# The first MoE's weight chunks in twos: one tile, one join and one check of 768 columns

## The chip, the core and the metric

The kernel runs on one core of one Trainium2 chip. The metric is the device time of one execution in microseconds (us), as the median over several runs. The engines are named as in the profile: PE is TensorE's matmuls, PEld its weight loads, DVE is VectorE, ACT ScalarE, POOL GpSimd and SP SyncE, which issues the transfers.

## The reference

Three stages follow each other: a gated linear attention, a first MoE with an RMS norm and a gated hidden layer, and a second MoE with a maximum of three products. The weights and `alpha` come as float64.

```python
for t in range(S):                       # S = 768, 4 x 8 heads of 48
    state = alpha[:, :, t, :, None] * state + np.einsum('bhd,bhe->bhde', k[:, :, t], v[:, :, t])
    y[:, :, t] = np.einsum('bhd,bhde->bhe', q[:, :, t], state)
...
xn = x / rms * rms_g                     # x: 3072 tokens of 384
g = xn @ w_gate                          # w_gate, w_val: 384 x 1536
silu = g * (1.0 / (1.0 + np.exp(-g)))
x = silu * (xn @ w_val) @ w_out          # w_out: 1536 x 384
...
h = np.maximum(np.maximum(x @ w1, x @ w2), x @ w3)   # 384 x 768 each
out = h @ w_out                          # 768 x 384
```

## The kernel before

**Attention.** The tokens are cut into 24 tiles of 128, worked on as a chunked recurrence. The first six tiles have `k`, `q` and `alpha` turned by PE (L579), the later ones by DVE (L585). A tile's *decay block* on DVE is the COPY `all`, a MEMSET, the scan `R`, `least` and `kT` (L604 to L613); later come `starts`, `aT`, `qT` (L617 to L630), the masked scores `at` (L666), the normed rows `xn` (L719) and the low half `xl` of the turned rows (L736), which with `xh` is what the first MoE reads.

**The first MoE** has 96 slots, each one block of 384 tokens by one hidden block of 128 columns. A slot is a gate product `g` (9 matmuls, L769), a value product `v` (L769), the silu on ACT into `sg` (L799), the multiply on DVE (L802), the high half `hh` on ACT (L806), the low half `hl` on DVE (L810) and the second product `s` on PE (L816). The first slots take hidden blocks 0 to 5 for token blocks 0 and 1, so the weights of a hidden block are wanted soon after the first gate. Every product is made of three matmuls of halves: high x high, high x low, low x high.

**The weights.** The class `Weights` cuts them into chunks of 128 partitions x 384 columns, three chunks (gate, value, out) for each hidden block, 36 for the first MoE (tag `w1`) and 24 for the second (`w2`). A chunk is loaded as int64 into a tile `raw` (L360, queue of SP), *joined* into a float32 tile `cv_t` by three integer operations on DVE (L58, L59, L60), split into a high half by a copy on ACT (L374) and a low half, the *rest*, by a subtraction on DVE (L380: `wgl`, `wvl`, `wol`), and *checked* on ACT by two activations with sums over the row (L389, L392, each with the read of its accumulator). Joins go two chunks at a time: `zip` over the two generators interleaves their operations.

```python
def join(nc, raw, t, n):
    yield nc.vector.tensor_scalar(bits, up, 3, TOP2 + 1, ALU.logical_shift_left, ALU.bitwise_or)
    yield nc.vector.scalar_tensor_tensor(bits, up, BELOW, bits, ALU.bitwise_or, ALU.bitwise_and)
    yield nc.vector.scalar_tensor_tensor(bits, low, 29, bits, ALU.logical_shift_right, ALU.bitwise_or)
```

**The order** of the instructions on each engine comes from the class `Order`. Every part is added with an engine, a cost, a due time (in slots), the parts that it needs, and the instructions that it issues. `run` plays the parts through: each engine that is free takes the ready part with the earliest due time, and is busy for the part's cost. The order in which the parts start is the order in the program. On PE, filler matmuls (L776) are put in where nothing is ready, until the first value product. So a cost that is changed can move any part of any engine against the others. For `w1` the raw tiles have four buffers: a load waits for the check and the join of the chunk four back.

Of the kernel before, what the change touches and what calls it, by code (L numbers as in the profile page):

```python
# [11 lines left out]
F32 = mybir.dt.float32  # L12
F32R = mybir.dt.float32r
BF16 = mybir.dt.bfloat16
I32 = mybir.dt.int32
U32 = mybir.dt.uint32
I64 = mybir.dt.int64
AF = mybir.ActivationFunctionType
# [7 lines left out]
P = 128  # L26
# [3 lines left out]
NF1 = F1 // P  # L30
# [16 lines left out]
def words(raw, n):  # L47

    bits, floats = (raw.bitcast(t).rearrange("p (n w) -> p n w", w=2) for t in (I32, F32))
    return bits[:, :n, 1], floats[:, :n, 1], bits[:, :n, 0]  # L50
# [231 lines left out]
def gla_moe_moe(ctx: ExitStack, tc: tile.TileContext, q, k, v, alpha, wg, wv, wo, g, w1, w2, w3, wo2, out):  # L282
    nc = tc.nc
# [5 lines left out]
    const = ctx.enter_context(tc.tile_pool(name="const", bufs=1))  # L289
    NSTAT = 4  # L290
    CW = 384
    tiles = [(b, c) for c in range(NC) for b in range(B)]
    nw = sum(w.shape[0] * w.shape[1] for w in (wg, wv, wo, w1, w2, w3, wo2)) // (P * CW)
    stats = const.tile([P, len(tiles) * NSTAT + nw], F32, name="stats")
    nc.gpsimd.memset(stats, 0.0)
    small = const.tile([P, nw], F32, name="small")
    nc.gpsimd.memset(small, 0.0)
    bound = const.tile([P, 1], F32, name="bound")
# [6 lines left out]
    NT = len(tiles)  # L305
# [3 lines left out]
    pp = work.enter_context(tc.tile_pool(name="pp", bufs=1, space=PSUM))  # L309
    banks = [pp.tile([P, 512], F32, name=f"bank{i}") for i in range(8)]  # L310
    mp = work.enter_context(tc.tile_pool(name="mp", bufs=2, side="left"))
    junk = const.tile([P, 512], BF16, name="junk")
    plan = Order()

    def bank(i, rows, a, n):
# [6 lines left out]
    class Weights:  # L322


        def __init__(self, tag, pool, bufs, chunks, where, due, needs):

            self.tag, self.pool, self.raws, self.tmps = tag, pool, {}, {}
            self.chunks, self.where = chunks, where
            n = len(chunks)
            first = tag == "w1"  # L330
            for i in range(n):
                at = due(i) - 10 - (HEAD[i // 2] if first and i < 8 else 1.5)
                before = needs(i) + self.prev("load", i, 1) + self.prev("check", i, bufs)
                if i >= bufs:
                    before.append((tag, "join", (i - bufs) // 2 * 2))
                plan.add((tag, "load", i), "SP", 1.1, at, before, partial(self.load, i, bufs), later=LAT)
            for i in range(0, n, 2):
                both = [j for j in (i, i + 1) if j < n]
                at = due(i) - (HEAD[i // 2] if first and i < 8 else 1 if first else 1.5)
                plan.add((tag, "join", i), "DVE", 1.3 * len(both), at,  # L340
                         [(tag, "load", j) for j in both] + self.prev("rest", i, 2) + self.prev("join", i, 2),
                         partial(self.join, both))
                plan.add((tag, "high", i), "ACT", 0.45 * len(both), at, [(tag, "join", i)] + self.needed(needs, both),
                         partial(self.high, both))
                plan.add((tag, "rest", i), "DVE", 0.47 * len(both), at + 0.2, [(tag, "high", i)],
                         partial(self.low, both))
                for j in both:
                    plan.add((tag, "check", j), "ACT", 1.42, at + 2, [(tag, "load", j)],
                             partial(self.check, j))

        def prev(self, kind, i, n):
            return [(self.tag, kind, i - n)] if i >= n else []
# [2 lines left out]
            return []  # L355

        def load(self, i, bufs):
            raw = self.pool().tile([P, CW], I64, name="raw", bufs=bufs)
            src, shape = self.chunks[i]
            nc.sync.dma_start(out=raw.rearrange("p (a b) -> p a b", a=shape[0]), in_=src)  # L360
            self.raws[i] = raw

        def join(self, both):
            steps = []
            for i in both:
                self.tmps[i] = self.pool().tile([P, CW], F32, name="cv_t", bufs=2)
                steps.append(join(nc, self.raws[i], self.tmps[i], CW))
            for _ in zip(*steps):
                pass
# [11 lines left out]
                    dl, self.tmps.pop(i).rearrange("p (a b) -> p a b", a=a), dh.bitcast(F32), ALU.subtract  # L381
                )

        def check(self, i):

            n = seen[0]
            seen[0] += 1
            col = NT * NSTAT + n
            nc.scalar.activation(  # L389
                junk[:, :CW], words(self.raws[i], CW)[1], AF.Square, scale=2.0**34, accum_out=stats[:, col:col + 1]  # L390
            )
            nc.scalar.activation(  # L392
                junk[:, :CW], junk[:, :CW], AF.Relu, scale=-(2.0**22), bias=bound, accum_out=small[:, n:n + 1]
            )

        def ready(self, i):
# [36 lines left out]
    for nm, fill in (("al", 1.0), ("kk", 0.0), ("qq", 0.0)):  # L433
        t = ap1.tile([P, 2 * H * 64], F32, name=f"in_{nm}")
# [352 lines left out]
    for s, (blk, f, pi) in enumerate(slots):  # L787
# [43 lines left out]
        if f == f1 - 1:  # L831
            for e in range(KT):
# [14 lines left out]
                before = [("yst", pi - 1, e)] if pi else []  # L847
                if f0:
                    plan.add(("yld", pi, e), "SP", 0.55, s - 1, before + [("yst", pi - 2, e), ("g", s - 1)] +
                             ([("yld", pi, e - 1)] if e else []), fetch, later=2.2)  # L850
                    before = [("yld", pi, e)]
# [51 lines left out]
        return tuple(w_[:, :, cols(f)] for w_ in w2s[kind])  # L903

    n = len(chunks1)
    done_att = [("t", "el", NT - 1), ("t", "sqb", NT - 1), ("w1", "check", n - 1), ("w1", "rest", n - 2)]

    class Weights2(Weights):
        def needed(self, needs, both):
# [8 lines left out]
    for blk in range(PLAIN):  # L918
# [5 lines left out]
        at = NS + (blk - 1) * NF2 + 1 if blk else NS - 6  # L924
# [7 lines left out]
        for i in range(KT):  # L932
# [8 lines left out]
            n = blk * KT + i  # L941
# [3 lines left out]
    for z in range(NZ):  # L945
# [31 lines left out]
        before = [("m", z - 1, 1) if z else ("mu", NS - 1), ("m", z - 1, 2) if z else None]  # L977
# [90 lines left out]
    for n in range(NS1):  # L1068
        fp, j = divmod(n, 3)
        at = NS + 3 + 0.5 * n  # L1070
# [6 lines left out]
        at = NS + 10.5 + 0.1 * n  # L1077
# [13 lines left out]
    for sb in range(1, NBLK // 2):  # L1091
# [211 lines left out]
        for late in range(2):  # L1303
            for t in range(2 * TPB):
# [18 lines left out]
                at = at0 + 8.4 + 0.33 * t + (2 * late)  # L1323
# [73 lines left out]
```

## Time and profile before

| | us |
|---|---|
| median of 3 runs | 892.62 (892.55 to 892.76) |
| the profiled execution | 892.83 |
| its span in the trace | 891.0 |
| PE busy | 871.4 (98%) |
| DVE busy | 639.5 (72%) |
| ACT busy | 363.6 (41%) |

The span runs from the first to the last instruction of the trace; what the run takes beyond it lies outside the trace. The granted clock of TensorE is given as a share of full speed. In rows of one engine's time line, the first number is the start in us from the span's start, the second the time from there to the end of the row's last instruction; x2 stands for two instructions in one row. A bracket at the end of a row is the idle time of the engine just before it and what ended it.

### The profile page before, as it was taken

What the parts mean: (1) busy time and instruction counts of PE and PEld (TensorE: products, weight loads), DVE (VectorE), ACT (ScalarE), POOL (GpSimd) and SP (SyncE); (2) the same over time, 40 slices, a digit from 0 to 9 for tenths busy, and PEclk for the clock granted to TensorE, in tenths of its full rate; (3) what the DMA queues carried; (4) which work ended last, traced back from release to release, by engine and by line L of the source; (5) the groups of instructions that cost most, each with busy time, mean ns of one, the idle gap of its engine ahead of it and who ended that gap; (6) DMA issues with size and microseconds to landing.
All of it is one profiled execution on the core that took longest, in us unless ns stands there. A gap on an engine that the chain in (4) does not pass through costs nothing.

```text
span 891.0 us, 16476 instructions
## 1 busy us (share of the span) xinstructions
PE 871.4 (98%) x6446; PEld 848.2 (95%) x6446; DVE 639.5 (72%) x1321; ACT 363.6 (41%) x928; POOL 22.1 (2%) x66
## 2 busy tenths in 40 slices
PE   7999899999999999999999999999999999999996
PEld 6889898999999999999999999999999999999996
DVE  8999999997666666666665367559886874865780
ACT  4578776433223333333233267645333232224121
POOL 1000000000000000000000000000000000000000
PEclk9999999999999999999999999999999999999998
DMA  9835654353222223222221025321200011011001
GB/s 201 190 105 175 194 164 139 86 142 85 56 53 77 53 50 81 52 53 80 58 59 51 5 85 178 107 94 49 81 1 28 1 54 54 1 53 54 1 1 56
DMA packets 106244, 69.17 MB, mean 78 GB/s; under 512 B 49200, under 2 KB 103856, under 8 KB 106160
## 3 DMA queue, kind: packets, MB, share of 16 engines
q1 hardware_dynamic: 106160, 68.05, 28.0%
q8 instruction: 52, 0.85, 0.4%
q14 instruction: 32, 0.26, 0.1%
HBM read 57.41 MB, written 10.62 MB: 76 GB/s over the span
## 4 chain that ended last, share of the span: by engine, by line
PE 86%; DVE 6%; DMA 3%; ACT 2%; SPq 2%; issue 1%; DVEq 0%; ACTq 0%
PE bank L769 35%; PE bank L1085 17%; PE bank L816 15%; PE bank L1313 6%; PE bank L653 2%; PE bank L691 2%; PE bank L776 2%; PE bank L972 2%; DMA raw<-in_moe_w_out_dram 1%; PE bank L685 1%; PE bank L676 1%; PE bank L725 1%; SPq L562 1%; DVE cv_t L59 1%; SPq L551 1%
## 5 line engine op out<-in xcount | busy, mean ns | idle before, releaser
L802 DVE TENSOR_TENSOR sg<-sg,bank 128x384 f32<-128x384 f32 x96 | 53.0, 552 | 95.7 <-PE bank L769 95.1
L806 ACT ACTIVATE hh<-sg 128x384 fp32r<-128x384 f32 x96 | 50.0, 521 | 149.0 <-DVE sg L802 148.9
L769 PE MATMUL bank<-xh,wgh 128*128 128x384 f32 x288 | 100.7, 349 | 1.5 <-ACT sg L799 1.5
L816 PE MATMUL bank<-hh,woh 128*128 128x384 f32 x288 | 98.0, 340 | 0.0
L816 PE MATMUL bank<-hl,woh 128*128 128x384 f32 x288 | 96.6, 335 | 1.3 <-DVE hl L810 1.2
L769 PE MATMUL bank<-xl,wgh 128*128 128x384 f32 x288 | 96.7, 336 | 1.2 <-DVE xl L736 1.2
L769 PE MATMUL bank<-xh,wgl 128*128 128x384 f32 x288 | 96.9, 336 | 0.2 <-DVE wgl L380 0.2
L769 PE MATMUL bank<-xh,wvh 128*128 128x384 f32 x288 | 96.7, 336 | 0.0
L769 PE MATMUL bank<-xh,wvl 128*128 128x384 f32 x288 | 96.4, 335 | 0.0
L816 PE MATMUL bank<-hh,wol 128*128 128x384 f32 x288 | 96.3, 334 | 0.0
L769 PE MATMUL bank<-xl,wvh 128*128 128x384 f32 x288 | 96.2, 334 | 0.0
L810 DVE TENSOR_TENSOR hl<-sg,hh 128x384 fp32r<-128x384 f32 x96 | 53.4, 556 | 31.0 <-ACT hh L806 30.9
L799 ACT ACTIVATE sg<-bank 128x384 f32<-128x384 f32 x96 | 46.7, 486 | 38.0 <-PE bank L769 36.9
L769 PEld LDWEIGHTS bank<-xh,wgh 128*128 128x128 f32 x288 | 54.1, 188 | 3.4 <-ACT sg L799 1.8
L816 PEld LDWEIGHTS bank<-hl,woh 128*128 128x128 f32 x288 | 54.1, 188 | 2.2 <-DVE hl L810 2.2
L816 PEld LDWEIGHTS bank<-hh,woh 128*128 128x128 f32 x288 | 54.0, 188 | 1.9
L769 PEld LDWEIGHTS bank<-xl,wgh 128*128 128x128 f32 x288 | 54.2, 188 | 1.5 <-DVE xl L736 1.5
L769 PEld LDWEIGHTS bank<-xh,wgl 128*128 128x128 f32 x288 | 54.1, 188 | 0.9 <-DVE wgl L380 0.9
L769 PEld LDWEIGHTS bank<-xh,wvh 128*128 128x128 f32 x288 | 54.1, 188 | 0.5 <-DVE sg L802 0.5
L769 PEld LDWEIGHTS bank<-xl,wvh 128*128 128x128 f32 x288 | 54.1, 188 | 0.0
L769 PEld LDWEIGHTS bank<-xh,wvl 128*128 128x128 f32 x288 | 54.1, 188 | 0.0
L816 PEld LDWEIGHTS bank<-hh,wol 128*128 128x128 f32 x288 | 54.0, 188 | 0.0
(252 smaller groups left out, 2058.0 us busy)
## 6 DMA issues: line engine op xcount, KB each, us to landing
raw<-in_moe_w_out_dram SPq DMA_DIRECT2D x18, 384.0 KB, 3.6
raw<-in_moe_w_dram SPq DMA_DIRECT2D x18, 384.0 KB, 3.8
y_scr<-yo SPq DMA_DIRECT2D x30, 192.0 KB, 1.9
raw<-in_moe_w_gate_dram SPq DMA_DIRECT2D x12, 384.0 KB, 4.2
vt<-in_v_dram SPq DMA_DIRECT2D x24, 192.0 KB, 2.6
raw<-in_moe_w_val_dram SPq DMA_DIRECT2D x12, 384.0 KB, 4.6
out_dram<-yo SPq DMA_DIRECT2D x24, 192.0 KB, 1.9
in_al<-in_alpha_dram SPq DMA_DIRECT2D x36, 96.0 KB, 2.2
```

The lines of the kernel that those rows point to most:

```text
L653: nc.tensor.matmul(self.sc[i][:, pr, :], self.kT[lo:hi, pr, :], self.qT[lo:hi, pr, :], start=True, stop=True)
L691: nc.tensor.matmul(self.y[tk, 2 * pr + i, :], at[i][:, pr, tk], vt[:, 2 * pr + i, :], start=not self.c, stop=True, skip_group_check=True,)
L769: nc.tensor.matmul(ps, w_[:, kt, col], m_[:, kt, :], start=i == 0, stop=i == 3 * KT - 1)
L776: nc.tensor.matmul(banks[4][:, 0:2 * P], ident.bitcast(BF16)[:, 0:P], mask.bitcast(BF16), start=True, stop=True)
L799: nc.scalar.activation(hid[s], banks[3][:, :NB], AF.Silu)
L802: nc.vector.tensor_tensor(hid[s], hid[s], banks[4][:, :NB], ALU.mult)
L806: nc.scalar.activation(hi_[s], hid[s], AF.Copy)
L810: nc.vector.tensor_tensor(lo_[s], hid.pop(s), hi_[s].bitcast(F32), ALU.subtract)
L816: nc.tensor.matmul(banks[e][:, :NB], w_[:, f, es], m_, start=f == f0 and i == 0, stop=f == f1 - 1 and i == 2)
L972: nc.tensor.matmul(banks[t][:, :DM], l_[:, tsl], r_[:, f, :], start=f == 0 and i == 0, stop=f == NF2 - 1 and i == 2)
L1085: nc.tensor.matmul(ps, l, r, start=start and i == 0, stop=i == 2, skip_group_check=True)
L1313: nc.tensor.matmul(banks[i][:, :DM], l, r[:, f, :], start=f == 0 and m_ == 0, stop=f == NF2 - 1 and m_ == 2)
```

## The change

For `w1` alone (`self.wide`), two chunks are loaded into the halves of one raw tile of 768 columns, of which there are two instead of four of 384. One join of three operations over 768 columns writes one `cv_t` of 768 columns, and one check runs over 768 columns. The copies to the high halves and the rests stay at 384. The first load of a pair waits for the check and the join of the pair before the last, the second load only for the first. The planner's cost of a pair's join goes from 2.6 to 2.25, that of its checks from 2 x 1.42 to 2.2, and the check waits for both loads. The tables of sums, `stats` and `small`, have 18 columns fewer. Lines behind L313 move down, from L360 on by 13 to 20 (L380 becomes L400, L604 becomes L624, L810 becomes L830).

```diff
+    nw -= NF1 * 3 // 2
...
-    junk = const.tile([P, 512], BF16, name="junk")
+    junk = const.tile([P, 2 * CW], BF16, name="junk")
...
-            first = tag == "w1"
+            first = self.wide = tag == "w1"
...
-                before = needs(i) + self.prev("load", i, 1) + self.prev("check", i, bufs)
+                before = needs(i) + self.prev("load", i, 1)
+                if not self.wide or i % 2 == 0:
+                    before += self.prev("check", i, bufs)
...
-                plan.add((tag, "join", i), "DVE", 1.3 * len(both), at,
+                plan.add((tag, "join", i), "DVE", 2.25 if self.wide else 1.3 * len(both), at,
...
+                if self.wide:
+                    plan.add((tag, "check", i), "ACT", 2.2, at + 2, [(tag, "load", j) for j in both],
+                             partial(self.check, i, 2 * CW))
+                    continue
...
+                if i % 2 == 0:
+                    self.raws[i] = self.pool().tile([P, 2 * CW], I64, name="raw", bufs=bufs // 2)
+                raw = self.raws[i - i % 2][:, i % 2 * CW:(i % 2 + 1) * CW]
...
+            if self.wide:
+
+                t = self.pool().tile([P, 2 * CW], F32, name="cv_t", bufs=1)
+                for _ in join(nc, self.raws[both[0]], t, 2 * CW):
+                    pass
+                for n, i in enumerate(both):
+                    self.tmps[i] = t[:, n * CW:(n + 1) * CW]
+                return
```

Two places in the order of DVE. The first is the start of the program, from the first tile's `qT` on; x2 stands for two equal rows, here one of each chunk. In before:

```order
L630 TENSOR_TENSOR qT<-bank_75,aT 112x512
L58 TENSOR_SCALAR cv_t<-raw 128x384 x2
L59 SCALAR_TENSOR_TENSOR cv_t<-raw,cv_t 128x384 x2
L60 SCALAR_TENSOR_TENSOR cv_t<-raw,cv_t 128x384 x2
L666 TENSOR_TENSOR at<-bank_78,mask 128x512
L666 TENSOR_TENSOR at<-bank_79,mask 128x512
L604 COPY all<-bank_80 112x4
L605 MEMSET bank_80 112x4
```

In the change, at the same place (L400 is the rest):

```order
L650 TENSOR_TENSOR qT<-bank_75,aT 112x512
L58 TENSOR_SCALAR cv_t<-raw 128x768
L59 SCALAR_TENSOR_TENSOR cv_t<-raw,cv_t 128x768
L60 SCALAR_TENSOR_TENSOR cv_t<-raw,cv_t 128x768
L686 TENSOR_TENSOR at<-bank_78,mask 128x512
L686 TENSOR_TENSOR at<-bank_79,mask 128x512
L400 TENSOR_TENSOR wgl<-cv_t,wgh 128x3x128
L400 TENSOR_TENSOR wvl<-cv_t,wvh 128x3x128
L624 COPY all<-bank_80 112x4
L625 MEMSET bank_80 112x4
```

The six operations of the join have become three, each reading the one before it, and the two rests of the first pair, which stood further back, have moved ahead of the second tile's decay block.

The second place is around the eleventh `hl` of the first MoE (slot 10), some 120 us into the span. In before, from that `hl` on:

```order
L810 TENSOR_TENSOR hl<-sg,hh 128x384
L380 TENSOR_TENSOR wgl<-cv_t,wgh 128x3x128
L380 TENSOR_TENSOR wvl<-cv_t,wvh 128x3x128
L58 TENSOR_SCALAR cv_t<-raw 128x384 x2
L59 SCALAR_TENSOR_TENSOR cv_t<-raw,cv_t 128x384 x2
L60 SCALAR_TENSOR_TENSOR cv_t<-raw,cv_t 128x384 x2
L802 TENSOR_TENSOR sg<-sg,bank_77 128x384
L604 COPY all<-aT 112x4
L605 MEMSET aT 112x4
L607 SCALAR_TENSOR_TENSOR R<-aT,ends 112x511
L612 TENSOR_SCALAR least<-R 112x4
L613 TENSOR_TENSOR kT<-kT,R 112x512
```

In the change, up to the same `hl`, which is the last row here:

```order
L624 COPY all<-aT 112x4
L625 MEMSET aT 112x4
L627 SCALAR_TENSOR_TENSOR R<-aT,ends 112x511
L632 TENSOR_SCALAR least<-R 112x4
L633 TENSOR_TENSOR kT<-kT,R 112x512
L822 TENSOR_TENSOR sg<-sg,bank_77 128x384
L400 TENSOR_TENSOR wgl<-cv_t,wgh 128x3x128
L400 TENSOR_TENSOR wvl<-cv_t,wvh 128x3x128
L58 TENSOR_SCALAR cv_t<-raw 128x768
L59 SCALAR_TENSOR_TENSOR cv_t<-raw,cv_t 128x768
L60 SCALAR_TENSOR_TENSOR cv_t<-raw,cv_t 128x768
L830 TENSOR_TENSOR hl<-sg,hh 128x384
```

The `hl` has moved behind a decay block, two rests and a join that followed it in before; the multiply in that stretch is the eleventh slot's own here and the next slot's there.

## Rows read from the trace of the kernel before

**Rows 1.** The page's head and its busy time by engine.
```profile
span 891.0 us, 16476 instructions
PE 871.4 (98%) x6446; PEld 848.2 (95%) x6446; DVE 639.5 (72%) x1321; ACT 363.6 (41%) x928; POOL 22.1 (2%) x66
```

**Rows 2.** Busy us by window: PE, PEld, DVE, ACT, POOL; clock, DMA share, GB/s.
```profile
49.00:156.00 107.00, 101.39 (x809) 96.05 (x809) 104.13 (x228) 78.57 (x217) 3.20 (x8) 1.00 0.55 161
200.00:884.00 684.00, 683.25 (x4726) 672.66 (x4724) 450.56 (x920) 239.88 (x582) 10.75 (x29) 1.00 0.19 55
```

**Rows 3.** What PE waited for from 49 us on: us, times, longest.
```profile
PE bank L769 <- ACT sg L799: 1.5, 1, 1.5
PE bank L816 <- DVE hl L810: 1.2, 1, 1.2
PE bank L769 <- DVE xl L736: 1.2, 1, 1.2
```

**Rows 4.** VectorE, one join: start, duration, row; idle before in brackets.
```profile
34.30 0.62 DVE L58 TENSOR_SCALAR cv_t<-raw 128x384 int32<-128x384 int32 x2
34.84 1.02 DVE L59 SCALAR_TENSOR_TENSOR cv_t<-raw,cv_t 128x384 int32<-128x384 int32 x2
35.77 1.02 DVE L60 SCALAR_TENSOR_TENSOR cv_t<-raw,cv_t 128x384 int32<-128x384 int32 x2
36.71 0.55 DVE L736 TENSOR_TENSOR xl<-bank,xh 128x384 fp32r<-128x384 f32 x1
```

**Rows 5.** VectorE, an operation that reads its predecessor's result, and one that doesn't.
```profile
38.24 1.22 DVE L607 TENSOR_TENSOR_SCAN R<-bank,ends 112x511 f32<-112x511 f32 x1
39.49 0.17 DVE L612 TENSOR_SCALAR least<-R 112x4 f32<-112x4 f32 x1
39.57 0.68 DVE L613 TENSOR_TENSOR kT<-bank,R 112x512 f32<-112x512 f32 x1
```

**Rows 6.** ScalarE from the first weight chunks on.
```profile
7.34 1.28 ACT L389 ACT_TABLE_LOAD   x1 [7.34 <-DMA raw<-in_moe_w_gate_dram]
10.67 0.58 ACT L389 ACTIVATE junk<-raw 128x384 bf16<-128x384 f32 x1 [0.60 <-DMA raw<-in_moe_w_val_dram]
11.90 0.19 ACT L392 ACTIVATION_READ_ACCUMULATOR junk<-junk,bound 128x1 f32 x1
15.06 0.55 ACT L389 ACTIVATE junk<-raw 128x384 bf16<-128x384 f32 x1 [1.08 <-DMA raw<-in_moe_w_out_dram]
16.78 0.51 ACT L374 ACTIVATE wgh<-cv_t 128x384 fp32r<-128x384 f32 x1
```

**Rows 7.** VectorE in the start-up.
```profile
14.72 0.15 DVE L604 COPY all<-bank 112x4 f32<-112x4 f32 x1
17.54 0.72 DVE L714 COPY S<-bank 48x192 f32<-48x192 f32 x2 [0.48 <-PE bank L676]
22.28 0.16 DVE L604 COPY all<-bank 112x4 f32<-112x4 f32 x1 [0.36 <-PE bank L579]
```

**Rows 8.** VectorE around the multiplies and the eleventh hl, 119 to 126.
```profile
119.17 0.57 DVE L810 TENSOR_TENSOR hl<-sg,hh 128x384 fp32r<-128x384 f32 x1
119.64 0.56 DVE L380 TENSOR_TENSOR wgl<-cv_t,wgh 128x384 fp32r<-128x384 f32 x1
122.97 0.55 DVE L802 TENSOR_TENSOR sg<-sg,bank 128x384 f32<-128x384 f32 x1
123.43 0.17 DVE L604 COPY all<-aT 112x4 f32<-112x4 f32 x1
125.71 0.55 DVE L810 TENSOR_TENSOR hl<-sg,hh 128x384 fp32r<-128x384 f32 x1
```

**Rows 9.** PE, where the eleventh hl is read.
```profile
122.07 0.33 PE L816 MATMUL bank<-hl,woh 128*128 128x384 f32 x1
```

**Rows 10.** VectorE and PE, the seventeenth hl.
```profile
154.10 0.55 DVE L810 TENSOR_TENSOR hl<-sg,hh 128x384 fp32r<-128x384 f32 x1
154.70 0.44 PE L816 MATMUL bank<-hl,woh 128*128 128x384 f32 x1 [1.20 <-DVE hl L810]
```

More of the change, by code (lines that the diff above doesn't have):

```diff
@@ L346, in __init__ @@
                          partial(self.low, both))
+                if self.wide:
+                    plan.add((tag, "check", i), "ACT", 2.2, at + 2, [(tag, "load", j) for j in both],
+                             partial(self.check, i, 2 * CW))
+                    continue
                 for j in both:
                     plan.add((tag, "check", j), "ACT", 1.42, at + 2, [(tag, "load", j)],
-                             partial(self.check, j))
+                             partial(self.check, j, CW))
         def prev(self, kind, i, n):
@@ L357, in load @@
         def load(self, i, bufs):
-            raw = self.pool().tile([P, CW], I64, name="raw", bufs=bufs)
             src, shape = self.chunks[i]
+            if not self.wide:
+                raw = self.raws[i] = self.pool().tile([P, CW], I64, name="raw", bufs=bufs)
+            else:
+                if i % 2 == 0:
+                    self.raws[i] = self.pool().tile([P, 2 * CW], I64, name="raw", bufs=bufs // 2)
+                raw = self.raws[i - i % 2][:, i % 2 * CW:(i % 2 + 1) * CW]
             nc.sync.dma_start(out=raw.rearrange("p (a b) -> p a b", a=shape[0]), in_=src)
-            self.raws[i] = raw
         def join(self, both):
             steps = []
+            if self.wide:
[5 more added lines that the diff above has]
+                return
             for i in both:
@@ L382, in low, with check @@
                 )
-        def check(self, i):
+        def check(self, i, n_):
             n = seen[0]
@@ L389, in check @@
             nc.scalar.activation(
-                junk[:, :CW], words(self.raws[i], CW)[1], AF.Square, scale=2.0**34, accum_out=stats[:, col:col + 1]
+                junk[:, :n_], words(self.raws[i], n_)[1], AF.Square, scale=2.0**34, accum_out=stats[:, col:col + 1]
             )
             nc.scalar.activation(
-                junk[:, :CW], junk[:, :CW], AF.Relu, scale=-(2.0**22), bias=bound, accum_out=small[:, n:n + 1]
+                junk[:, :n_], junk[:, :n_], AF.Relu, scale=-(2.0**22), bias=bound, accum_out=small[:, n:n + 1]
             )
@@ L905, in gla_moe_moe @@
     n = len(chunks1)
-    done_att = [("t", "el", NT - 1), ("t", "sqb", NT - 1), ("w1", "check", n - 1), ("w1", "rest", n - 2)]
+    done_att = [("t", "el", NT - 1), ("t", "sqb", NT - 1), ("w1", "check", n - 2), ("w1", "rest", n - 2)]
     class Weights2(Weights):
```

## The prediction

> **What bounds the kernel now.** I read the page's head first: TensorE (PE) is busy 98% of a span of 891.0 us, VectorE (DVE) 72%, ScalarE (ACT) 41% [rows 1]. The profiled execution took 892.83 us, so 1.83 us lie outside the span; the median of the plain runs is 892.62, 0.21 below, and I add my difference to the median. A share of 72% is an average, so the next view is the busy time by window [rows 2]. From 200 to 884 us PE is busy 683.25 of 684 us, at full clock, and DVE 450.56: nothing that DVE saves there can move the end. From 49 us, where the first gate product of the first MoE starts, to 156 us, DVE is busy 104.13 of 107 us: in this stretch VectorE is full, idle for 2.87 us in all, since attention and the conversion of the first MoE's weights share it. PE is the longer chain even there, and it stops only where an operation of DVE or ACT comes late. The view of PE's waits gives the three largest: 1.2 us for `xl` (L736), 1.5 us for the silu's `sg` (L799), 1.2 us for an `hl` (L810) [rows 3]. So the end moves by what the change does to PE's waits before 156 us, and by nothing else: PE's remaining work is the same, as all 96 slots and the second MoE keep their matmuls. The 23 filler matmuls fewer (L776) stand before the first value product, where PE waits for DVE anyway.
>
> **The change, part by part.**
>
> *The join.* Two narrow joins are interleaved, two operations of 384 columns in each of three rows, and the pair lasts from 34.30 to 36.71, 2.41 us, until the next operation starts [rows 4]. Interleaved, each operation reads what the one before its predecessor wrote. The wide join is a chain of three: each reads what its predecessor wrote. Rows 5 show what that costs: the operation at 39.49 reads the scan's result and starts 0.03 us after the scan's end (38.24 + 1.22 = 39.46), while the one at 39.57 needs nothing of its predecessor and starts 0.09 before its end (39.49 + 0.17 = 39.66). The trace has no operation of 768 columns. Bounds: not below half of a pair's rows (as if width were free, 1.2 us), not above the sum of the durations of all six (0.35 + 0.35 + 4 x 0.55 = 2.9 us). Nearest rows: a tensor-tensor operation lasts 0.68 us at 512 columns [rows 5] and 0.55 to 0.57 at 384 [rows 8], so 0.12 per 128 columns, and 0.55 + 3 x 0.13 = 0.94 at 768; the rows of two, 0.62 and 1.02, less the one overlap of 0.08, give 0.54 and 0.94 as well. Chain: 0.54 + 0.03 + 0.94 + 0.03 + 0.94 - 0.08 = 2.40 us. I take that: **no gain for DVE**, 0.00 ± 0.02 a pair. What the three fewer operations save in overlap, the two dependent starts take back.
>
> The Trainium skill ("VectorE: DVE Perf Modes", sections "The DRAIN you can't avoid" and "Rules for kernel authors") says that between operations chained on this engine semaphores cost nothing extra, and that the number of operations is what to reduce. By that the chain would cost 0.54 + 0.94 + 0.94 - 3 x 0.08 = 2.18 us, 0.23 less a pair; rows 5 speak against it, since the dependent start there stands 0.12 us behind an independent one. It is the first rival below.
>
> *The check.* One narrow check lasts from 10.67 to 12.09, 1.42 us [rows 6], a pair 2.84. A wide one lies between 1.42 and 2.84; two activations of twice the width and half of the accumulator reads make me take 2.2. That saves 0.6 x 18 = 11 us of ACT, which has 28 us idle between 49 and 156 [rows 2]: worth nothing by itself. The price is in the start-up: the table load, which now runs when the first chunk has landed (7.34), waits for the second too, as 10.67 does now [rows 6].
>
> *Start-up.* 10.67 + 1.28 (table) + 2.2 = 14.15 for the first check's end, against 12.09: 2.06 later. The three small checks behind it end now at 15.06 - 1.08 = 13.98, then at 16.04; the copies `wgh` and `wvh` behind them (0.51 each) end at about 17.0, and the second rest (0.55) at about 17.5. The order of DVE now has both rests (L400) directly behind them and ahead of the turned tile's COPY (first pair of order rows). That COPY goes from 14.72 to about 17.5, +2.8; the two rests are gone from further back (-0.93), and the idle 0.48 and 0.36 us there [rows 7] are swallowed: **+1.0 us** on DVE. Bounds: 0, if an early gap hides it, and 2.1.
>
> *The order.* The planner's smaller costs (2.25 for a join, 2.2 for a check) move DVE's operations against each other. The one that counts is the eleventh `hl`. In before it stands ahead of two rests, a join and a decay block of a turned tile; in the change behind them all (second pair of order rows). By rows 8 these last 122.97 - 119.64 = 3.33 and 125.71 - 123.43 = 2.28 us, 5.6 together. So this `hl`, done at 119.17 + 0.57 = 119.74 in before, is done at 119.74 + 5.6 + 1.0 + 0.2 (fourteen joins at the upper edge of my 0.02) = 126.5. PE reads it at 122.07 [rows 9], and what PE does ahead of that product is the same in both orders but for the fillers. **PE is 4.5 us late there.** Cover gone: 122.07 - 119.74 = 2.3 us hid the `hl`'s time before. Part of the delay shows earlier, since `wvl` of the sixth hidden block stands behind three transposes of a new tile now, but a delay of PE counts once: the latest bound holds. The `xl` wait of rows 3 lies ahead of this point and is inside it.
>
> *After it.* At the seventeenth `hl` only one pair of rests more stands ahead of it (0.93), with 0.2 to 0.4 for the joins and 1.0 of the start: 2.3 later, so done at 154.10 + 0.55 + 2.3 = 157.0. PE would have wanted it at 154.70 - 1.20 = 153.5 [rows 10] and now wants it at 158.0: that wait of 1.2 goes. From there every multiply has only the joins' 0.5 us or less more ahead, and PE is the bound again.
>
> *Loads.* Each pair's two transfers are issued when both halves are free, so the first goes later and the second earlier; the join needed both anyway. Nothing, but the silu that waited 1.5 us behind a check [rows 3] may meet another such wait.
>
> **Sum.** +4.5 - 1.2 = +3.3, if no wait takes the place of the last one; +4.5, if one of its size does. Planned orders on a full DVE leave such waits somewhere, so I take the middle: **+3.9, 896.5 us**.
>
> **The rivals.**
>
> *Fewer operations save time: faster.* Mechanism: dependent wide operations overlap like independent ones and cost less than the slope says. It must shorten the join enough that the eleventh `hl` comes by 122.07: 4.5 us over fourteen joins, 0.32 us each, so 2.09 us or less against 2.41. From that point PE meets no delay there and loses the waits for `xl` and `hl`, 2.4 us: 890.2. For it: DVE is full, and 54 operations go. Against it: rows 5, by which dependent operations don't overlap, and the slope of rows 4, 5 and 8.
>
> By the rule of the Trainium skill on chained operations above ("VectorE: DVE Perf Modes") fourteen joins would give back 14 x 0.23 = 3.2 of the 4.5 us, short of that point.
>
> The Trainium skill ("Perfetto Trace Analysis", "Optimizing Scalar/DVE Operations") recommends grouping into larger operations where the engine is saturated, with about 60 ns of overhead for a DVE operation on SBUF. By that estimate 54 operations are worth 3.2 us, and the time would be about 889.4.
>
> *No change: slack swallows it.* DVE's 2.87 us of idle time [rows 2] and a start-up that costs nothing take 3.9 off the 4.5; what remains pays with the wait of 1.2 that goes: 892.0 to 893.5. Against it: DVE idles where PE or a transfer is late, and a later PE is no help there.
>
> *Waits stack: slower still.* Checks that wait for two landings hold silus and `hh` behind them on ACT, once or twice at the 1.5 us of rows 3, and the wait at 154.70 comes back: +4.5 + 1.5 + 1.2, so 899 to 900. For it: ACT is in order and already stopped PE so once. Against it: a wide check is 0.6 us shorter than two.
>
> **How the numbers follow.** My forecast 0.60, stacked waits 0.13, no change 0.14, faster 0.13. The forecast's own range is 894.2 (1.9 us of DVE's idle swallowed, +1.6) to 898.2. Of the rivals I include the stacked waits and the upper part of no change: 893.0 to 899.6. A change of 0.2% (1.8 us) is about what a measurement of this kernel can tell from none: faster 0.13, same 0.15, slower 0.72.
>
> **What would show it.** Wide joins of 2.38 to 2.45 us from first start to the next free start; the check at about 2.2; the table load at about 10.6; PE waiting for a rest near 92 us or for the `hl` near 126, for several us; no wait for `hl` near 158; and from 200 us on a PE as busy as now. Wrong: joins of 2.2 us or less, DVE idle over 5 us between 49 and 160, or a PE that passes the eleventh `hl` before 124.

## The result and the profile after

The change is slower: 898.08 us median (896.53 to 899.39, 5 runs) against 892.76 (892.55 to 893.09, 5 runs), 1.0056 times before, 95% interval 1.0043 to 1.0069. The forecast was 896.5, 893.0 to 899.6. A second set of runs of it, among the experiments, gave 1.0049 (1.0035 to 1.0063). The total came out near the forecast, but two of its terms were wrong in size and two more were missing; they partly cancel, so the nearness is in part luck.

The profiled execution of the change took 898.23 us. The first lines of its page, to set beside [rows 1]:

```profile
span 896.5 us, 16264 instructions
PE 870.9 (97%) x6423; PEld 847.5 (95%) x6423; DVE 639.1 (71%) x1267; ACT 351.6 (39%) x856; POOL 23.4 (3%) x66
```

Its busy time by window, in the columns of [rows 2]:

```profile
49.00:156.00 107.00, 96.93 (x748) 91.74 (x746) 97.33 (x168) 67.44 (x157) 3.63 (x8) 0.95 0.53 157
200.00:889.00 689.00, 687.60 (x4769) 677.24 (x4768) 457.85 (x935) 241.30 (x587) 11.43 (x31) 1.00 0.20 56
```

What the reader is to see: from 200 us on PE is as full as before, but between 49 and 156 us PE is busy 96.93 of 107 us in place of 101.39, DVE 97.33 in place of 104.13, and the granted clock of TensorE is 0.95 in place of 1.00. DVE now idles 9.7 us where it idled 2.9. The forecast named over 5 us there as a sign against itself, and rightly.

What PE waited for from 45 us on, to set beside [rows 3]:

```profile
PE bank L789 <- ACT sg L819: 2.9, 2, 2.1
PE bank L789 <- DVE wvl L400: 2.6, 1, 2.6
PE bank L666 <- DVE aT L640: 2.3, 1, 2.3
PE bank L696 <- ACT kn L679: 0.9, 1, 0.9
```

`aT`, `kn` and `xn` stop PE longer, `wvl` stops it for 2.6 us, the silu's `sg` twice. The waits for `xl` at 92 and for the `hl` near 154 are gone, as forecast. Two of the longest waits in PE's time line, with some of the rows around them:

```profile
91.18 0.34 PE L789 MATMUL bank<-xl,wvh 128*128 128x384 f32 x1
94.09 0.44 PE L789 MATMUL bank<-xh,wvl 128*128 128x384 f32 x1 [2.57 <-DVE wvl L400]
94.54 0.34 PE L789 MATMUL bank<-xl,wvh 128*128 128x384 f32 x1
...
95.53 0.52 PE L789 MATMUL bank<-xh,wvl 128*128 128x384 f32 x1
95.85 0.52 PE L789 MATMUL bank<-xh,wgh 128*128 128x384 f32 x1
...
98.36 0.34 PE L789 MATMUL bank<-xh,wgl 128*128 128x384 f32 x1
98.54 0.33 PE L836 MATMUL bank<-hh,woh 128*128 128x384 f32 x1
...
128.41 0.44 PE L789 MATMUL bank<-xh,wgh 128*128 128x384 f32 x1 [2.12 <-ACT sg L819]
```

The time from start to start is 0.17 to 0.18 us at full speed (98.36 to 98.54) and 0.32 us from 95.53 to 95.85: 0.8 us after the wait of 2.57 us PE's clock falls to half and stays there for ten matmuls, 3.2 us. The same follows the wait that ends at 128.41, and there is such a stretch from 65 to 67 us, after the wait of 2.26 us for `aT`. In this execution 26 matmuls of the first MoE start 0.32 us apart in place of 0.17: 26 x 0.147 = **3.8 us** that no wait shows. In before's trace not one does from 49 us on, where its longest wait is 1.5 us [rows 3]. The windows by themselves show the clock (the last three numbers are clock, DMA share and GB/s):

```profile
88.00:94.00 6.00, 3.52 (x21) 3.20 (x19) 5.97 (x9) 4.26 (x11) 0.00 (x0) 1.00 0.32 98
95.00:98.00 3.00, 3.00 (x11) 3.00 (x10) 2.90 (x5) 0.55 (x2) 0.00 (x0) 0.50 0.44 100
99.00:105.00 6.00, 6.00 (x37) 6.00 (x36) 4.59 (x9) 1.77 (x4) 0.00 (x0) 1.00 0.91 252
```

At 95 to 98 us it is 0.50, the lower of the two levels, 1.2 of 2.4 GHz.

The wide join and the start-up on DVE, to set beside [rows 4] and [rows 7]:

```profile
16.77 0.56 DVE L400 TENSOR_TENSOR wgl<-cv_t,wgh 128x384 fp32r<-128x384 f32 x1 [1.77 <-ACT wgh L394]
17.71 0.16 DVE L624 COPY all<-bank 112x4 f32<-112x4 f32 x1
...
87.36 0.55 DVE L58 TENSOR_SCALAR cv_t<-raw 128x768 int32<-128x768 int32 x1
87.94 0.96 DVE L59 SCALAR_TENSOR_TENSOR cv_t<-raw,cv_t 128x768 int32<-128x768 int32 x1
88.94 0.96 DVE L60 SCALAR_TENSOR_TENSOR cv_t<-raw,cv_t 128x768 int32<-128x768 int32 x1
89.81 0.55 DVE L822 TENSOR_TENSOR sg<-sg,bank 128x384 f32<-128x384 f32 x1
```

The wide join lasts from 87.36 to 89.81, 2.45 us, against 2.41 for the two narrow ones. The dependent starts stand 0.03 us and more behind their predecessor's end (87.36 + 0.55 = 87.91, next 87.94); the independent row at 89.81 stands 0.09 ahead (88.94 + 0.96 = 89.90). The second COPY of DVE starts at 17.71 in place of 14.72, behind a rest that waited 1.77 us for `wgh`.

On ScalarE the first wide check lasts from 12.29 to 14.42 (14.23 + 0.19), 2.13 us. A later one, and the eleventh `hl` behind it, to set beside [rows 8] and [rows 9] (rows of ACT, DVE and PE):

```profile
125.51 0.91 ACT L409 ACTIVATE junk<-raw 128x768 bf16<-128x768 f32 x1 [3.33 <-DMA raw<-in_moe_w_gate_dram]
127.38 0.19 ACT L412 ACTIVATION_READ_ACCUMULATOR junk<-junk,bound 128x1 f32 x1
127.89 0.47 ACT L819 ACTIVATE sg<-bank 128x384 f32<-128x384 f32 x1
128.01 0.56 DVE L830 TENSOR_TENSOR hl<-sg,hh 128x384 fp32r<-128x384 f32 x1
131.28 0.52 PE L836 MATMUL bank<-hl,woh 128*128 128x384 f32 x1
```

The `hl` is done at 128.57, and PE reads it at 131.28 without waiting for it: PE had been stopped before, at 128.41, by the silu's `sg` behind this check.

The second MoE, whose code the change leaves alone, went the other way. From the last second product of the first MoE (600.49 in before, 608.96 in the change) to the last matmul (883.77 and 889.75) before takes 283.28 us and the change 280.79. So 8.5 us are lost ahead of that point, and **2.5 us come back** behind it.

### The profile page after: what moved, and what is told of

Read it like the earlier page. It is cut to its first block, busy times and chain, and to the rows that moved or that the text cites. A ratio compares the mean times of both kernels' runs of the same rounds, so it can differ in the third digit from the quotient of the medians.

```text
span 896.5 us, 16264 instructions
## 1 busy us (share of the span) xinstructions
PE 870.9 (97%) x6423; PEld 847.5 (95%) x6423; DVE 639.1 (71%) x1267; ACT 351.6 (39%) x856; POOL 23.4 (3%) x66
## 4 chain that ended last, share of the span: by engine, by line
PE 83%; DVE 10%; DMA 2%; issue 2%; ACT 1%; SPq 0%; DVEq 0%; ACTq 0%
PE bank L789 34%; PE bank L1105 17%; PE bank L836 15%; PE bank L1333 6%; PE bank L673 2%; PE bank L711 2%; PE bank L992 2%; PE bank L796 1%; PE bank L705 1%; DVE cv_t L59 1%; PE bank L696 1%; DMA raw<-in_moe_w_gate_dram 1%; DVE cv_t L58 1%; DVE cv_t L60 1%; PE bank L745 1%
## 5 line engine op out<-in xcount | busy, mean ns | idle before, releaser
L830 DVE TENSOR_TENSOR hl<-sg,hh 128x384 fp32r<-128x384 f32 x96 | 53.3, 555 | 31.8 <-ACT hh L826 31.8
```

Source lines behind the costliest of these rows:

```text
L830: nc.vector.tensor_tensor(lo_[s], hid.pop(s), hi_[s].bitcast(F32), ALU.subtract)
```

## The experiments

The ratios are to runs of before on the same chip, with 95% intervals.

### The order with narrow operations

The change's raw tiles, plan and order (DVE, PE and SP row by row), but before's join and checks, and before's sizes of the tables.

```diff
+                for n, i in enumerate(both):
+                    self.tmps[i] = t[:, n * CW:(n + 1) * CW]
+                    steps.append(join(nc, self.raws[both[0]][:, n * CW:(n + 1) * CW], self.tmps[i], CW))
+                for _ in zip(*steps):
+                    pass
...
+            if n_ > CW:
+                for j in (0, 1):
+                    self.narrow(self.raws[i][:, j * CW:(j + 1) * CW], CW)
+                return
```

> The change's order of instructions on DVE, PE and SP and its raw tiles of 768 columns, but with before's narrow operations: two interleaved joins of 384 columns and two narrow checks for a pair. If the order is the cause, the time stays at 896.5 to 899.5 us and PE waits for `wvl` near 93 us and for an `sg` near 128 us again; only the start-up gets about 1 us back. If the wide operations are the cause, it falls to 892.8, and the join takes 2.41 us a pair instead of 2.45. The tables in front of the other tiles have before's sizes here: if the place of the tiles sets the pace of the second MoE's matmuls (0.1755 us in before, 0.1733 in the change), these last 2.3 us longer than in the change.

Measured: 895.53 us, 1.0022 (1.0014 to 1.0031). Its second MoE takes 283.30 us, as before's. PE waits 2.53 us for `wvl` at 91.85 and 1.41 for an `sg` at 123.88, so these waits belong to the order; but the time lies between the two answers. The order is part of the loss and not all of it.

### The wide operations in the old order

```diff
+        def both(self, i, n_):
+            if i % 2:
+                self.check(i - 1, 2 * CW)
...
-                plan.add((tag, "join", i), "DVE", 2.25 if self.wide else 1.3 * len(both), at,
+                plan.add((tag, "join", i), "DVE", 1.3 * len(both), at,
```

> The change's wide loads, joins and checks, but put where the plan of before has them: the order of DVE, PE and SP is that of before, row by row; the wide check stands where the second check of its pair stood. If the order is the cause, the waits of 2.1 to 2.6 us on PE don't come and the time is 892.8 plus eighteen joins at 0.04 us more, at most 0.7, plus up to 1 us for the start-up that waits for two landings: 893 to 894.5, and 890.7 to 892.2 if the second MoE keeps the change's faster pace. If wide operations cost it, about 898.

Measured: 896.92 us, 1.0040 (1.0026 to 1.0055), from 893.10 to 899.82. That is not what the theory of the order expects: in the very order of before the wide operations are slower by about as much as the whole change. Run again:

> The old order with the change's wide loads, joins and checks once more, for its spread (893.1 to 899.8 before) and a second profile. If transfers that land at different times are behind the spread, this profile differs from the first in the idle time that ends with a landing on ACT or DVE, and PE's waits and half-speed stretches follow; if not, the two profiles wait in the same places for other reasons.

Measured: 895.48 us, 1.0033 (1.0023 to 1.0044). The two profiles, with spans of 891.3 and 892.8 us, wait in the same places. The second has the first pair's second landing later (the table load starts at 11.43 in place of 10.87) and five of the first MoE's matmuls at half speed near 70 us in place of none. Both profiles are of the shortest execution of their set, so they do not show what the longer ones do. The clock of the whole span, which is known for every execution, goes with the time in the first set: 0.997 or 0.998 in the five up to 895.07 us, 0.994 to 0.996 in the seven from 896.70 us on. In the second set it goes with it only weakly, so the cause of the spread stays open.

### The place of the tiles

```diff
-    junk = const.tile([P, 512], BF16, name="junk")
+    junk = const.tile([P, 696], BF16, name="junk")
```

> Before, with `junk` made 368 bytes a partition longer, by which the change moves the tiles that follow it; nothing else. If the place of the tiles sets the pace of the second MoE, its matmuls go from 0.1755 to 0.1733 us apart and the time falls by about 2.3 us to 890.5. If the pace comes from elsewhere (the order, or the code's place in memory), the time stays at 892.8.

Measured: 891.22 us, **0.9973** (0.9964 to 0.9983). One group of the second MoE's first products, first in before, from 669 to 860 us:

```profile
L1085 PE MATMUL bank<-xh,w1h 128*128 128x384 f32 x45 | 15.2, 339 | 0.0
```

and of this kernel:

```profile
L1085 PE MATMUL bank<-xh,w1h 128*128 128x384 f32 x45 | 15.0, 334 | 0.0
```

A matmul of the group lasts 339 ns in before and 334 here. In before the groups of these products (L1085) lie between 334 and 343 ns, here all are at 334, and the second MoE takes 280.83 us in place of 283.28. Another 368 bytes a partition in a table, which nobody reads, make the kernel 2.4 us faster; what they change is the place of all tiles behind it. Every kernel here with that shift (two have 8 bytes more) takes 280.8 to 281.0 us for this stage, and both without it 283.3. Why one place is slower was not found. This version is faster than before and than the change.

### The planner's old costs

```diff
-                plan.add((tag, "join", i), "DVE", 2.25 if self.wide else 1.3 * len(both), at,
+                plan.add((tag, "join", i), "DVE", 1.3 * len(both), at,
...
-                    plan.add((tag, "check", i), "ACT", 2.2, at + 2, [(tag, "load", j) for j in both],
+                    plan.add((tag, "check", i), "ACT", 2.84, at + 2, [(tag, "load", j) for j in both],
```

> The change with the planner's costs left at 2.6 for a join and 2 x 1.42 for a check, so that only these two numbers differ from the change; the order that comes out is a third one, with the first wide check still one part. If the order decides, the time can land anywhere from 891 to 898, by the waits on PE that its trace shows, at the same 2.45 us for a join; if the wide operations decide, it stays at 898.

Measured: 893.97 us, 1.0006 (0.9995 to 1.0016). With the wide operations, a third order is 2.4 to 3 us better than the old one and some 4 better than the change's. So two numbers of the planner take back most of what the change lost, with every wide operation kept. It shows how much the order can do, not which of its rows does it.

### One wide operation at a time, in the old order

Three kernels with the order of DVE, PE and SP of before and tiles in the change's place: pairs of loads with a wide check and narrow joins (interleaved as in the first experiment); with a wide join and narrow checks, as below; and with both narrow.

```diff
+        def both(self, i, n_):
+            self.narrow(self.raws[i - i % 2][:, i % 2 * CW:(i % 2 + 1) * CW], CW)
```

> As the run with the old order of DVE, PE and SP and the change's wide operations (median 896.9), but the join narrow and interleaved again; loads in pairs and the wide check stay. The same run without any of the three took 891.2 with the tiles at this place. If the wide check is what costs (it holds ACT until both halves have landed, at the start and later), 895 to 897 with the same spread of several us; if the join is, about 891.5.

> The old order, loads in pairs, the join wide, but two narrow checks where before has them. If the chain of dependent wide operations is what costs, 18 joins at 0.04 us give 0.7 on a full DVE, so 892 to 893; if a wide join costs more by making the first high copy wait for the whole pair, up to 895; if the check is the cause, 891.5.

> The old order with narrow joins and narrow checks; only the raw tiles are pairs, two of 768 columns in place of four of 384, so that both halves come free together. If the later first load of a pair matters, checks and joins wait longer for their transfers and the time is 893 to 896; if not, 891.2.

Measured: the check alone 894.60, 1.0015 (1.0004 to 1.0027); the join alone 891.97, 0.9991 (0.9982 to 1.0000); pairs alone 891.69, 0.9987 (0.9978 to 0.9995). Against 0.9973 for the moved tiles, pairs cost 0.0014, 1.3 us; a wide join on top of them 0.0004, 0.4 us; **a wide check 0.0028, 2.5 us**; both together (1.0033 and 1.0040) 4.1 to 4.7 us. Of these steps only the check, and both together, are clear of the intervals; those of pairs and moved tiles overlap, and so do those of pairs with and without the wide join. So the check is the larger part. That with the join it costs more than the two apart is not shown: the intervals of the check alone and of both overlap too.

One place where it costs is seen in ScalarE's time line. With narrow operations, the second check of a pair and the next `xh`:

```profile
20.63 0.55 ACT L416 ACTIVATE junk<-raw 128x384 bf16<-128x384 f32 x1 [1.41 <-DMA raw<-in_moe_w_gate_dram]
21.83 0.19 ACT L419 ACTIVATION_READ_ACCUMULATOR junk<-junk,bound 128x1 f32 x1
23.77 0.47 ACT L759 ACTIVATE xh<-bank 128x384 fp32r<-128x384 f32 x1
```

and with the wide check alone:

```profile
20.90 0.92 ACT L415 ACTIVATE junk<-raw 128x768 bf16<-128x768 f32 x1 [1.42 <-DMA raw<-in_moe_w_gate_dram]
24.72 0.47 ACT L758 ACTIVATE xh<-bank 128x384 fp32r<-128x384 f32 x1
```

In the first the last landing ends the wait at 20.63, and 1.4 us of check follow (to 21.83 + 0.19), because the first half was checked while the second was on its way. In the second all of the wide check stands behind the last landing, and `xh` starts 24.72 - 20.90 = 3.8 us after it in place of 23.77 - 20.63 = 3.1. DVE's `xl` waits for `xh`; its waits up to 156 us, in the kernel with the wide check (us in total, times, longest; the one with narrow checks has no such line):

```profile
DVE xl L762 <- ACT xh L758: 1.2, 3, 0.7
```

Where the time goes is read from PE, whose order is the same in both. The first gate product of the first MoE, with pairs alone and then with the wide check:

```profile
49.28 0.45 PE L796 MATMUL bank<-xh,wgh 128*128 128x384 f32 x1
50.51 0.44 PE L795 MATMUL bank<-xh,wgh 128*128 128x384 f32 x1
```

So 1.2 us are lost ahead of it. The difference is 2.7 us where PE reads the third slot's `hl` (78.9 and 76.1 us), after seven more matmuls at half speed (fourteen from 69 to 74 us, with pairs alone seven), and 2.5 us at the last second product (604.74 and 602.28). In these two executions no check behind the third slot costs anything in the end. The second landing of the first pair was 0.8 us later in the one with the wide check (11.48 against 10.69), so not all of the 1.2 us need be the check's.

### The first check narrow

```diff
+            if i < 2:
+                self.narrow(self.raws[0][:, i * CW:(i + 1) * CW], CW)
```

> The old order with the change's wide loads, joins and checks, but the first pair checked in two narrow operations, so that ScalarE's table load and first check need the first landing alone. If the start-up is what the wide check costs, the time falls from 1.0035 times before (two runs) to that of the wide join alone, 0.999; if the seventeen later wide checks cost it (each holds ACT 2.1 us and waits for both halves), it stays at 1.003.

Measured: 897.61 us, 1.0052 (1.0039 to 1.0066): nothing gained, if anything lost. The table load starts at 7.64 again, but ScalarE then waits at the next check:

```profile
22.15 0.91 ACT L419 ACTIVATE junk<-raw 128x768 bf16<-128x768 f32 x1 [3.90 <-DMA raw<-in_moe_w_gate_dram]
26.47 0.56 DVE L766 TENSOR_TENSOR xl<-bank,xh 128x384 fp32r<-128x384 f32 x1 [2.32 <-ACT xh L762]
```

It waits 3.90 us for the second landing of the next pair, `xh` stands behind it, and DVE waits 2.32 for `xh`. PE's first gate product:

```profile
53.15 0.45 PE L799 MATMUL bank<-xh,wgh 128*128 128x384 f32 x1
```

That is 3.9 us later than with pairs alone, and at the last second product it is 3.8 us (606.10 and 602.28): in this execution, of 895.66 us, all of the loss stands ahead of the first gate product, where the second pair's check is, and none behind it. The landing that it waited for was itself 1.4 us later than in the old order's first profile with all checks wide (22.15 against 20.74), so the check and the landing are not told apart. The same in the order of the change:

```diff
+            if n_ > CW and i == 0:
+                for j in (0, 1):
+                    self.narrow(self.raws[0][:, j * CW:(j + 1) * CW], CW)
+                return
```

> The change, with its own order of DVE, PE and SP, and the first pair alone checked in two narrow operations. By the start-up theory DVE's second COPY comes about 2 us earlier (17.71 in the change, 15.61 with narrow operations), PE's wait for `wvl` near 92 us shrinks by as much, and the time falls from 898 by 2 to 3 us; if the later checks are the cause, by less than 1 us.

Measured: 896.45 us, 1.0032 (1.0021 to 1.0043), against 1.0049 for the change beside it: 1.5 us better by the ratios, 0.2 by the medians (896.45 and 896.69), and the intervals overlap. Its COPY starts at 16.52, not the 15.61 of the narrow kernel. Its first gate product stands at 46.44, against 47.96 in the change's second profile, but its last second product at 606.55, against 606.31: 18 of its matmuls ran at half speed behind the waits for `wvl` and `sg`, some 2.6 us. So the start-up costs 1.5 us up to the first gate product in the change's order; that they reach the end is not shown. The first check is not the cause in the old order.

### The order alone, tiles in place, and the change again

> The change's order with narrow joins and checks, as in the first run of it (1.0022 times before), and the tables lengthened by 368 bytes, so that the tiles lie where the change has them. The second MoE's pace goes to 0.1733 us and the time to 1.0022 - 0.0027 = 0.9995 times before, 893.1; then the order alone, against 0.9987 for the old order with pairs, costs 0.7 us. If the place of the tiles and the order act on each other, it differs from that.

```diff
-    junk = const.tile([P, 512], BF16, name="junk")
+    junk = const.tile([P, 696], BF16, name="junk")
```

(in the kernel of the first experiment). Measured: 892.91 us, 1.0001 (0.9992 to 1.0010), where 0.9995 was expected, which lies in the interval.

> The change itself once more, beside the three others: 1.0056 times before, with a spread of 3 us. A second profile shows whether PE again waits for `wvl` near 94 us and for an `sg` near 128 us, and whether its matmuls again run at half speed behind each of them.

Measured: 896.69 us, 1.0049 (1.0035 to 1.0063). Its profile, of 896.27 us, waits in the same places, with other lengths (2.46 us for `kn` at 69.06 in place of 0.92), and has no half-speed stretch behind the wait for `wvl`, which is shorter:

```profile
94.33 0.44 PE L789 MATMUL bank<-xh,wvl 128*128 128x384 f32 x1 [2.19 <-DVE wvl L400]
95.00:98.00 3.00, 3.00 (x19) 3.00 (x18) 2.93 (x5) 0.32 (x1) 0.00 (x0) 1.00 0.53 139
```

The clock is 1.00 from 95 to 98 us where it was 0.50 in the other execution of the same kernel (after 2.57 us of waiting there, 2.19 here). The wait for `aT` is as long in both, 2.26 us, and the clock after it is not the same. The wait and the clock from 65 to 67 us, in the first profile and then in the second:

```profile
62.14 0.60 PE L666 MATMUL bank<-ident,kT 112*128 112x112 f32 x4 [2.26 <-DVE aT L640]
65.00:67.00 2.00, 2.00 (x7) 2.00 (x8) 1.93 (x3) 0.00 (x0) 0.00 (x0) 0.50 0.06 16
62.35 0.60 PE L666 MATMUL bank<-ident,kT 112*128 112x112 f32 x4 [2.26 <-DVE aT L640]
65.00:67.00 2.00, 1.60 (x9) 1.28 (x8) 1.90 (x4) 0.19 (x1) 0.00 (x0) 1.00 0.14 50
```

The second has its half-speed stretch behind the wait for `kn`, 0.50 from 69.5 to 72 us, among attention's matmuls. So a part of the 3 us between runs of the change is the clock.

## Why the prediction came out right, and where its steps were wrong

Set beside each other, as ratios to before: tiles moved 0.9973; with pairs, 0.9987; with the new order, 1.0001; with the wide operations, 1.0049 and 1.0056. In us of 893: **-2.4** for the place, **+1.3** for pairs, **+1.3** for the order, **+4.3 to +4.9** for the wide operations in that order; +4.4 to +5.0 in all. The old order gives 4.1 to 4.7 for the wide operations, so between these two orders the terms nearly add. Of the steps, the place and the wide operations are clear of the intervals; those of pairs and of the order are not. And the wide operations need not cost this much: in the third order, of the planner's old costs, the kernel with all of them takes 1.0006. The forecast put all of its +3.9 on the order, with 1.0 for the start-up and 0.2 for the joins inside it; that terms of other sizes and signs add up to nearly the same is luck.

*The join: right.* Forecast 2.40 us and no gain for DVE, measured 2.45: a dependent start behind the predecessor's end takes back what the fewer operations save. It is 0.04 longer a pair and, alone, 0.4 us in the end, within the noise.

*The check: the step that failed.* "Worth nothing by itself" went by the sum of its time, 2.84 to 2.2 (2.13 measured, 12.29 to 14.42). What the rest of ScalarE's queue sees is the time from the last landing to the check's end, and that grows from 1.4 to 2.1 us, since nothing is done while the second half is on its way. Eighteen times `xh`, `kn`, silus and `hh` can stand behind it. In its sum the forecast priced that at the first check alone; at the later ones it is what the rival of stacked waits named. Alone, in the old order, the check measured 2.5 us, and there the profiles show the loss within the first 80 us. In the change's order a later one, at 125.51, stops PE as well.

*The order: mis-sized.* The forecast had +4.5 at the eleventh `hl`, and -1.2 later. The order alone, with narrow operations, costs 1.3 us, against a forecast of +3.3 to +4.5 with start-up and joins. It brings PE's wait for `wvl`, behind three transposes (2.05 us at 91.81 with narrow operations, 2.57 in the change), and one for an `sg`. At the eleventh `hl` PE was stopped before, at 128.41, by a silu behind a check that waited 3.33 us for a landing, and read the `hl` at 131.28, 9.2 us later than in before and not 4.5; so the bound that the sum rested on never held. It did not hold with narrow operations either: there the `hl` was done at 124.36 and PE came to it at 125.36. The stop by a silu was the mechanism of the rival of stacked waits, which had 0.13.

*Start-up: right in size at its place.* COPY at 17.71, forecast 17.5. PE's first gate product comes 1.8 to 2.0 us later with the wide operations than with narrow ones in the same order (47.75 and 47.96 against 45.92), near the forecast's upper bound of 2.1. What of it reaches the end is not shown: two kernels differ by 1.5 us by the ratios, and their intervals overlap.

*The loads: put at nothing.* Pairs alone measured 1.3 us, with intervals that overlap.

*Missing: the clock.* Waits of 2.1 to 2.6 us were each followed by 3 us at half speed in the profiled execution of the change, 3.8 us. The forecast let the end move by PE's waits "and by nothing else", and counted them at their length only. The second profile of the change shows that it need not happen behind each of them.

*Missing: the place of the tiles.* -2.4 us, through sizes of tables that the diff changes in passing; the forecast held PE's remaining work to be the same. Without that gain the change would have been slower by 0.8%.

The rival that fewer operations make the kernel faster fell: the wide join took 2.45 us, not 2.09 or less. The Trainium skill's sentence that a semaphore between chained operations costs nothing extra ("VectorE: DVE Perf Modes", "The DRAIN you can't avoid") does not hold for these rows, if a dependent start is read as such a semaphore: by the prediction's estimate from it the join would have taken 2.18 us. The rival of no change fell with the interval. One bound of the prediction does not follow from its working: the lower end of its own range is given as +1.6, but +3.9 less 1.9 is +2.0 and +3.3 less 1.9 is +1.4; nothing rests on it.

Open: which of the later checks costs how much in the change's order, whether check and join together cost more than apart, whether pairs alone cost anything, and what the longer executions of the old order do, which no profile shows. No run here separates them.

## What to carry to other kernels

An operation that joins two inputs must wait for the later one: price it by the time from the last landing to its end, not by its busy time, and look at who stands behind it on the same engine. Two interleaved chains hide each other's dependent starts; one wide chain does not, so halving the number of operations can leave the time where it was. And before a small difference is explained by the edit, lengthen a table by what the edit shifts the tiles and measure that alone.

## What the runs showed of the hardware that was not expected

Matmuls of one group of the second MoE lasted 339 or 334 ns with nothing changed but 368 bytes a partition that nobody reads and that move the tiles in SBUF: 283.3 or 280.8 us for the stage. And the granted clock of TensorE fell to 0.50 for about 3 us behind a wait of 2.57 us, stayed 1.00 behind one of 2.19 us at the same place in the same kernel, and stayed 1.00 behind all of before's from 49 us on, up to 1.5 us. The length of the wait alone does not decide it: behind 2.26 us for `aT` it fell in one profile of the change and not in the other. And with pairs alone seven matmuls ran at half speed from 68 to 70 us, just behind attention's small matmuls, where the waits before were 0.85 and 0.31 us; in before, with the same two waits, none did.
